# One engine per result slot in the last stage, and three queues for a closing store

## The chip, the cores and the metric

The kernel runs on one core of one Trainium2 chip. The core has TensorE (matrix multiplication into PSUM), VectorE, ScalarE, GpSimd and SyncE, which work in parallel, each on its own queue of instructions, and 16 DMA engines that move data between the device memory and the on-chip memory SBUF. The metric is the device time of one execution in microseconds (us), given as the median of several runs.

In the rows of the profile PE is TensorE, PEld its weight loads, DVE is VectorE, ACT ScalarE, POOL GpSimd and SP SyncE. A q behind the name (SPq, POOLq) is that engine's sequencer, which also issues transfers.

## What is computed

For an input `x` of 2048 positions by 640 channels the reference blends two branches with a gate per position:

```python
g = _sigmoid((x * gate_w).sum(-1, keepdims=True))
a = _A_ref(x, A_wqkv, A_wo)          # dilated sliding-window attention, 32 heads, window 8, projected by wo
b = _B_ref(x, B_A_re, ..., B_Dskip)  # state-space kernel K[d, l], long convolution of x with K by FFT, + x * Dskip
return g * a + (1 - g) * b
```

The last operation concerns us: `g * a` has been computed and stored earlier, the long convolution `b` comes out of the last inverse transform, and `(1 - g) * b + g * a` is formed and stored as bf16.

## The kernel before

The first and longest part computes the gate, the attention branch and the convolution kernel. It leaves `g * a` in a scratch tensor `gaS` in device memory and `1 - g` in `omS`. The second part is `fft_conv` (from line 987): it transforms both factors of the convolution, multiplies the spectra on VectorE, and transforms back in two steps. The step before the last (line 1075) fills slots `cp` in PSUM, which ScalarE and VectorE empty in turn through the helper `evict` (lines 490 to 494) into `C`, a view of the buffer `bufA`.

The last stage is the loop that begins at line 1084. The 32 values of an index `v` are split into ten groups of three and one of two, n = 0 to 10. For each group TensorE fills a PSUM slot `yp` (24 matmuls for three values, line 1105). The slot takes two PSUM banks, and there are four slots. Of each group:

- the first value is finished by VectorE in one fused instruction (`both`, line 1121): it reads the slot, multiplies by `1 - g` (a scalar per partition, `om32`), adds `g * a` (`gaF`) and writes the result tile `ot`;
- the other values are scaled by ScalarE (`scale`, line 1114): one instruction per value reads the slot, multiplies by `1 - g` and writes a tile `tt` in SBUF;
- VectorE then adds `g * a` to the values in `tt` (`mix`, line 1118, one instruction for both values) and writes them to `ot`.

Both engines thus read every slot. A tile `ot` has room for six values and there are four such buffers. Groups 0, 9 and 10 have a tile of their own; groups 1 and 2, 3 and 4, 5 and 6, 7 and 8 share one. When a tile is complete, it is stored in four transfers, one for each 32 partitions: two issued by SyncE and two by GpSimd (line 1132). A transfer of six values moves 120 KB, of three 60 KB, of two 40 KB.

The order of the instructions on each engine is set by a small planner (class `Plan`, lines 69 to 204). Every step is added with an engine, an assumed duration, the steps it depends on, the slots it takes (`acq`) and frees (`rel`) and a due time. The planner simulates the engines with these durations and writes the steps in the order found. On each engine that order is then fixed; the waits between engines and on transfers are put in by the framework, from which tiles an instruction reads and writes.

Of the kernel before, what the change touches and what calls it, by code (L numbers as in the profile page):

```python
# [10 lines left out]
ACT = mybir.ActivationFunctionType  # L11
ALU = mybir.AluOpType
AX = mybir.AxisListType
F32 = mybir.dt.float32
BF16 = mybir.dt.bfloat16
# [5 lines left out]
S = 2048  # L21
D = 640
# [14 lines left out]
def _attn_consts():  # L37
# [5 lines left out]
    for wp in range(W):  # L43
# [7 lines left out]
            v=[299.2, -444.8, 725.4, 80.9, 775.3, 1122.6, -30.6, 686.6], g=[-162.9, 197.0, 381.2, -256.7, -603.2, -606.7, -146.9, -1.6, 186.6, -1231.8, -442.2],  # L51
# [860 lines left out]
def _fft_consts():  # L912
    w = lambda e: np.exp(-2j * np.pi * e / NF)
    t1 = np.arange(32); t2 = np.arange(64); f1 = np.arange(32); f2 = np.arange(64)
    F1 = w(64 * np.outer(t1, f1 + 0.5))
    f1c = np.zeros((32, 32, 2), np.float32)
    f1c[:, :, 0] = F1.real; f1c[:, :, 1] = F1.imag
    f1b = np.zeros((4, 32, 4, 64), np.float32)
    for g in range(4):
        f1b[g, :, (0, 2, 1, 3)[g], :] = f1c.reshape(32, 64)  # L920
    f1c = f1b.reshape(128, 256)
    Phi = w(t2[None, :, None] * (f1[:, None, None] + 0.5 + 64 * f2[None, None, :]))
    phis = np.zeros((64, 2, 32, 3, 2, 64), np.float32)
    for c2 in range(2):
        phis[:, c2, :, 0, c2, :] = Phi.real.transpose(1, 0, 2)
        phis[:, c2, :, 1, c2, :] = Phi.imag.transpose(1, 0, 2)
        phis[:, c2, :, 2, c2, :] = -Phi.imag.transpose(1, 0, 2)
    phis = phis.reshape(128, 32, 3, 128)
    G = np.conj(w(64 * np.outer(f2, t2)))
    ga = np.concatenate([G.real, G.imag], axis=1)  # L930
    gb = np.concatenate([-G.imag, G.real], axis=1)
    gab = np.stack([ga, gb], axis=1)
    gab = np.concatenate([gab, gab], axis=0).astype(np.float32)
    Psi = np.conj(w((64 * t1[None, None, :] + t2[:, None, None]) * (f1[None, :, None] + 0.5))) * (2.0 / NF)
    psis = np.stack([Psi.real, -Psi.imag], axis=-1).transpose(1, 0, 3, 2)
    ps = np.zeros((2, 2, 32, 64, 2, 2, 32), np.float32)
    for e in range(2):
        ps[:, e, :, :, :, e, :] = psis[None]
    psis = ps.reshape(128, 64, 2, 64)
    return f1c.astype(NPBF), phis.astype(NPBF), gab.astype(NPBF), psis.astype(NPBF)  # L940
# [47 lines left out]
def fft_conv(ctx, tc, P, big, Bu, gaS, out2d):  # L988
    nc = tc.nc
    _, _, _, psi_np = _fft_consts()  # L990
# [7 lines left out]
    om32 = sb.tile([128, 32], F32, name="om32")  # L998
    psi = sb.tile([128, 64, 2, 64], BF16, name="psi")
    nc.vector.tensor_copy(om32[:], omF[:])  # L1000
    gaF = P["pool"].tile([128, 32, 320], BF16, name="gaF", tag="uga")
    gr = gaS.rearrange("(a j v) (e c) -> j e a v c", j=2, v=32, e=2)
    orr = out2d.rearrange("(a j v) (e c) -> j e a v c", j=2, v=32, e=2)
    phis, q = P["phis"], {}
    a, b, c = ExitStack(), ExitStack(), ExitStack()
    wk = a.enter_context(tc.tile_pool(name="ff_wk", bufs=2, side="right"))
    q["ps"] = b.enter_context(tc.tile_pool(name="ff_ps2", bufs=2, space=PSUM))
    pl = Plan(free=dict(P=0.0, A=0.0, D=0.0, S=0.0, G=0.0), phase=0.0, look=0.0, ba=0.0, bd=0.0, grace=0.0, warm=1)
    ends, muls = [], {}
    for fb in range(8):  # L1010
        spec, sp = {}, {}
        for n, (nm, ro) in enumerate((("k", 0), ("k", 1), ("u", 0), ("u", 1))):
# [17 lines left out]
            d = 5.2 * fb + 1.3 * n  # L1030
            m = pl.add(f"fp{fb}{nm}{ro}", "P", 1.18, trans, acq=["fp"], due=d)
            e = sp[nm, ro] = pl.add(f"sp{fb}{nm}{ro}", "A", 1.17, ev, deps=[m], rel=[("fp", m)], due=d)
# [10 lines left out]
        t = {}  # L1043
# [12 lines left out]
        for k, (x0, x1) in enumerate(((0, 16), (16, 48), (48, 80)) if fb == 7 else ((0, 80),)):  # L1056
            w = 0.04 + 0.0096 * (x1 - x0)
# [5 lines left out]
    cps, prev = [], None  # L1063
    for cb in range(20):
        ms = []
        for ro in range(2):
# [10 lines left out]
            prev = pl.add(f"inv{cb}{ro}", "P", 0.27, inv, deps=[muls[cb, ro]], after=ends + [prev], acq=["cy"] if ro == 0 else [], due=60 + cb + 0.1 * ro)  # L1077
# [2 lines left out]
        def ev(en, cb=cb):  # L1080
            evict(nc, en, C.rearrange("p x (c q) -> p x c q", c=2)[:, :, :, 4 * cb:4 * cb + 4], q["cp", cb][:].rearrange("p c l x -> p x c l"))
        cps.append(pl.add(f"cp{cb}", "AD", {"A": 1.0, "D": 1.18}, ev, deps=ms, rel=[("cy", ms[0])], due=60 + cb))
    prev, v0 = None, 0
    for n, w in enumerate((3,) * 10 + (2,)):
        vs = range(v0, v0 + w)
        v0 += w
        sole = n in (0, 9, 10)
        if sole or n % 2:
            os, o = [], {"v": vs[0], "n": 0}
        k0 = o["n"]  # L1090
        o["n"] += w

        def fin(_, n=n, vs=vs, o=o, k0=k0):
            if n == 0:
                a.close(); big.close(); c.close()
                q["yps"] = ctx.enter_context(tc.tile_pool(name="ff_ps4", bufs=4, space=PSUM))
                q["wk"] = ctx.enter_context(tc.tile_pool(name="ff_wk2", bufs=4, side="right"))
            if k0 == 0:
                o["t"] = q["wk"].tile([128, 6, 320], BF16, name="ot")
            yp = q["yp", n] = q["yps"].tile([128, 2, 512], F32, name="yp")  # L1100
            for k, v in enumerate(vs):
                for ro in range(2):
                    for j in range(2):
                        for h in range(2):
                            nc.tensor.matmul(yp[64 * j:64 * j + 64, h, 160 * k:160 * k + 160], psi[64 * h:64 * h + 64, 32 * j + v, ro, :], C[64 * h:64 * h + 64, 64 * ro + 32 * j + v, :],
                                             start=(ro == 0), stop=(ro == 1), skip_group_check=True, tile_position=(64 * h, 64 * j))

        def part(k, n=n):
            return q["yp", n][:, :, 160 * k:160 * k + 160]

        def scale(_, v, k, n=n, part=part):
            if k == 1:
                q["tt", n] = q["wk"].tile([128, 2, 320], BF16, name="tt")
            nc.scalar.activation(q["tt", n][:, k - 1, :].rearrange("p (h d) -> p h d", h=2), part(k), ACT.Identity, scale=om32[:, v:v + 1])  # L1114

        def mix(_, n=n, vs=vs, o=o, k0=k0):
            w = len(vs)
            nc.vector.tensor_tensor(o["t"][:, k0 + 1:k0 + w, :], q["tt", n][:, 0:w - 1, :], gaF[:, vs[1]:vs[0] + w, :], ALU.add)  # L1118

        def both(_, v=vs[0], o=o, k0=k0, part=part):  # L1120
            nc.vector.scalar_tensor_tensor(o["t"][:, k0, :].rearrange("p (h d) -> p h d", h=2), part(0), om32[:, v:v + 1], gaF[:, v, :].rearrange("p (h d) -> p h d", h=2), ALU.mult, ALU.add)  # L1121
        m = prev = pl.add(f"yp{n}", "P", 0.20 * w, fin, deps=cps, after=[prev] + (ends + list(muls.values()) if n == 0 else []), acq=["yp"], due=100 + n)
        os.append(pl.add(f"st{n}", "D", 0.47, both, deps=[m], rel=[("yp", m)], due=100 + n))
        tts = []
        for k in range(1, w):
            tts.append(pl.add(f"tt{n}{k}", "A", 0.44, lambda _, f=scale, v=vs[k], k=k: f(_, v, k), deps=[m], acq=["tt"] if k == 1 else [], rel=[("yp", m)], due=100 + n))
        os.append(pl.add(f"mx{n}", "D", 0.46, mix, deps=tts, rel=[("tt", tts[0])], due=100 + n))
        if sole or n % 2 == 0:
            def store(e, o=o):
                for h in range(2):  # L1130
                    j = (0, 2)[e == "G"] + h
                    (nc.sync if e == "S" else nc.gpsimd).dma_start(orr[j // 2, j % 2][:, o["v"]:o["v"] + o["n"], :], o["t"][32 * j:32 * j + 32, 0:o["n"]])  # L1132
            for e, t_ in (("S", 1.3), ("G", 1.1)):
                pl.add(f"out{n}{e}", e, t_, store, deps=os, due=100 + n, dma=0.12 * o["n"])
    pl.emit(tc)


# [5 lines left out]
def gated_mix_kernel(ctx, tc, A_x, A_wqkv, A_wo, B_A_re, B_A_im, B_B_re, B_B_im, B_C_re, B_C_im, B_log_dt, B_Dskip, gate_w, out):  # L1143
# [47 lines left out]
    with c2:  # L1191
# [70 lines left out]
        for n in range(2 * HC):  # L1262
            first("fk", lambda: half[1, "kc"], Bk[:, HC:], n, half[1, "ld"] + [cst], kg.pqs + xdone, pr["u0"] - 50.0 + n)
        pl.emit(tc)
    fft_conv(tc, P, big, now["big"][:].rearrange("p (c f q g) -> p c f q g", c=NCH, f=64, q=8), gaS, o2)


# [50 lines left out]
```

## Time and profile before

| | |
|---|---|
| median of 3 runs | 378.2 us (378.02 to 378.23) |
| the profiled execution | 377.12 us, span 375.1 us |
| busy share: TensorE, VectorE, ScalarE, GpSimd | 84%, 85%, 82%, 26% |
| start of the last stage's matmuls | 354.82 us |
| last result written by VectorE | 369.34 us |
| end of the span | 375.1 us |

The span is the time from the first to the last instruction of the profiled execution; its run took 2.0 us more than its span. A row of the timeline gives start, duration, engine, line, operation, output and inputs, count, and in brackets the idle time before it with what ended that. A row of the groups gives the count, the busy time and the mean of one in ns, then the idle time before them. A row of the windows gives a stretch of the span, the busy time and count of each engine, TensorE's granted clock, the busy share of the DMA engines and the GB/s that they moved.

### The profile page before, as it was taken

To read this page: it belongs to the slowest core of one execution; us is meant where nothing else is said; L and a number is where in the kernel's file an instruction comes from. 1 tells how busy PE (TensorE), PEld (TensorE's weight loads), DVE (VectorE), ACT (ScalarE), POOL (GpSimd) and SP (SyncE) were. 2 spreads that over 40 slices of the span, in tenths; PEclk is the share of its full clock that TensorE was granted. 3 is DMA by queue.
4 is the path that set the end of the run, shared out by engine and by line. 5 is a ranking of instruction groups with operands and counts; after the bars stand their busy time and mean duration, and the time that the engine had idled before them with its cause. 6 is when DMAs were issued, how large, how long until landed. Compare 5 with 4: busy or idle time off the path is not lost. (4 is left out here: it accounts for less than half of the span.)

```text
span 375.1 us, 11789 instructions
## 1 busy us (share of the span) xinstructions
PE 315.3 (84%) x5066; PEld 186.9 (50%) x5094; DVE 320.1 (85%) x436; ACT 307.3 (82%) x415; POOL 95.7 (26%) x129
## 2 busy tenths in 40 slices
PE   0159999998999999979888979999999899997840
PEld 0135664434444455544444445556776665656730
DVE  4698999759999887998999999999897478998872
ACT  1598985389998898897998899997886799996872
POOL 8930450230102113293540201000010032200044
PEclk9998999999999999995969999999999999998995
DMA  8991799671416539605557751311372059932055
GB/s 262 370 252 55 227 284 270 175 231 33 146 62 190 184 101 252 142 17 127 143 127 243 194 187 58 120 56 48 126 249 78 35 134 243 217 79 46 3 135 149
DMA packets 44424, 56.71 MB, mean 151 GB/s; under 512 B 23716, under 2 KB 36580, under 8 KB 44116
## 3 DMA queue, kind: packets, MB, share of 16 engines
q0 software_dynamic: 8112, 28.75, 26.2%
q1 hardware_dynamic: 34804, 26.69, 26.1%
q8 instruction: 40, 0.66, 0.7%
q10 hardware_dynamic: 1456, 0.52, 0.6%
q14 instruction: 12, 0.10, 0.1%
HBM read 36.17 MB, written 19.77 MB: 149 GB/s over the span
## 5 line engine op out<-in xcount | busy, mean ns | idle before, releaser
L330 PE MATMUL tb<-bufA 128*128 128x512 bf16 x283 | 71.2, 388 | 4.5 <-DVE bufA L494 2.3
L772 PE MATMUL ar<-Rarg,L 64*128 64x304 bf16 (+1 forms) x480 | 55.8, 288 | 11.0 <-ACT big L784 4.7
L784 ACT ACTIVATE big<-ar 128x608 bf16<-128x608 int16 x96 | 58.3, 682 | 3.1 <-PE ar L772 2.5
L379 DVE TENSOR_TENSOR prod<-qc,kc 128x2048 bf16<-128x2048 bf16 x40 | 47.4, 1219 | 3.7 <-PE lg L385 3.1
L444 DVE TENSOR_TENSOR pv<-vc,asb 128x2048 bf16<-128x2048 bf16 x40 | 47.3, 1219 | 3.3 <-PE tb L449 3.3
L786 ACT ACTIVATE big<-ar 128x864 bf16<-128x864 f32 x60 | 49.3, 895 | 0.7 <-PE ar L772 0.4
L330 PEld LDWEIGHTS <-bufA 128*128 128x128 bf16 x300 | 33.2, 120 | 31.6 <-issue 6.8
L772 PEld LDWEIGHTS <-L 64*128 64x128 bf16 x480 | 22.3, 95 | 41.8 <-issue 38.0
L449 PE MATMUL tb<-pv,ident 128*128 128x512 bf16 (+1 forms) x181 | 39.7, 356 | 1.0 <-issue 0.5
L825 PE MATMUL kps<-qq,pt 128*32 128x22 bf16 (+1 forms) x2560 | 36.8, 174 | 0.7 <-issue 0.6
L825 PEld LDWEIGHTS <-pt 128*32 128x32 bf16 (+1 forms) x2560 | 25.0, 93 | 23.9 <-issue 15.3
L1021 PEld LDWEIGHTS <-PHI 128*128 128x128 bf16 x256 | 24.8, 97 | 17.7 <-issue 8.3
L492 ACT ACTIVATE prj<-tb 128x512 bf16<-128x512 f32 x27 | 16.0, 598 | 13.8 <-PE tb L330 13.4
L466 PE MATMUL tb<-wo_sb,oT 128*128 128x320 bf16 x160 | 27.2, 300 | 0.0
L449 PEld LDWEIGHTS <-ident 128*128 128x128 bf16 x192 | 18.2, 101 | 14.4 <-issue 2.2
L492 ACT ACTIVATE sp_k<-fp 128x1280 bf16<-128x1280 f32 x16 | 19.4, 1236 | 3.0 <-PE fp L1021 2.5
L245 PE MATMUL ar<-ident,xn 128*128 128x128 bf16 x80 | 7.9, 263 | 16.0 <-DMA xn<-in_A_x_dram 14.3
L809 DVE TENSOR_TENSOR qq<-big 128x1408 bf16<-128x1408 bf16 x24 | 21.2, 884 | 0.0
L1021 PE MATMUL fp<-bufA,PHI 128*128 128x320 bf16 x128 | 19.4, 298 | 2.1 <-ACT sp_u L492 1.2
L1021 PE MATMUL fp<-big,PHI 128*128 128x320 bf16 x128 | 19.5, 298 | 1.6 <-ACT sp_k L492 1.3
L492 ACT ACTIVATE sp_u<-fp 128x1280 bf16<-128x1280 f32 x16 | 19.4, 1236 | 1.6 <-PE fp L1021 1.2
L968 POOL COPY pace<-Usb 32x2 bf16<-32x2 bf16 x7 | 13.2, 1883 | 23.9 <-DMA Usb<-in_A_x_dram 23.9
(168 smaller groups left out, 595.9 us busy)
## 6 DMA issues: line engine op xcount, KB each, us to landing
asb<-aS SPq DMA_DIRECT2D x8, 512.0 KB, 3.9
PHI<-c_phi POOLq DMA_DIRECT2D x8, 384.0 KB, 4.9
Sprm<-pc SPq DMA_DIRECT2D x12, 240.0 KB, 7.6
L<-Sprm SPq DMA_DIRECT2D x80, 36.0 KB, 3.3
kc<-kS POOLq DMA_DIRECT2D x8, 337.5 KB, 6.3
vc<-vS POOLq DMA_DIRECT2D x8, 337.5 KB, 5.2
xn<-in_A_x_dram SPq DMA_DIRECT2D x4, 640.0 KB, 11.6
qc<-qS POOLq DMA_DIRECT2D x8, 320.0 KB, 6.0
```

The source lines that it names most:

```text
L330: nc.tensor.matmul(ppf, self.wq[:, kt, which * D + e:(which + 1) * D:5], self.xT[:, c0 // 1024, kt, c0 % 1024:c0 % 1024 + SC], start=(kt = ...
L379: nc.vector.tensor_tensor(b[e][:], b["qc"][:, e, :].unsqueeze(1).to_broadcast([128, W, C]), win(b["kc"][:, e, :], 0, W, DIL, C), ALU.mult)
L444: nc.vector.tensor_tensor(b["pv", e][:, :, k, :].rearrange("p w (b t) -> p w b t", t=64), for_e, aw, ALU.mult)
L449: nc.tensor.matmul(b["op", e][:, 0:n, :], ident[:], b["pv", e][:, w, 0:n, :], start=(w == 0), stop=(w == W - 1))
L466: nc.tensor.matmul(apf[:, :320], b["oT"][:, e, i * 128:(i + 1) * 128], wo_sb[:, e, hf * 320:(hf + 1) * 320], start=(e == 0), stop=(e == 4))
L492: nc.scalar.activation(o, i, ACT.Identity)
L772: nc.tensor.matmul(ar[:, g2, a0:a0 + ncol], L[rows, sb, gp, l0:l0 + 128], R[rows, c0:c0 + ncol], start=True, stop=True, tile_position=(64 ...
L784: nc.scalar.activation(dst[:, 2 * gp:2 * gp + 2, sub, :], ar[:].bitcast(I16)[:, :, 0:2 * SW:2], ACT.Sin, scale=SCL)
L786: nc.scalar.activation(dst[:, 2 * gp:2 * gp + 2].rearrange("p g s n -> p g (s n)"), ar[:, :, 0:2 * EW], ACT.Exp)
L809: nc.vector.tensor_tensor(qq[:], trg[:, :, KI:].rearrange("p a (v m) -> p a v m", v=2), exq[:, :, KI:].unsqueeze(2).to_broadcast([128, 32, ...
L825: nc.tensor.matmul(kps[32 * g:32 * g + 32, h, NM * ql:NM * ql + NM], pt[rows, k, v, :], qq[rows, k, v, :], start=(g not in started), stop= ...
L1021: nc.tensor.matmul(fp[:, fl, 0:320].rearrange("p (c x) -> p c x", x=32), phis[fb][:, fl, kind, :], B[:, :, 2 * f1 + ri].rearrange("p c q g ...
```

## The change

A slot is emptied by one engine alone. ScalarE takes groups 0, 2, 3, 5, 6, 8 and 9: it scales all three values into a `tt` tile that is now three values wide, and VectorE adds `g * a` to the three in one instruction. VectorE takes groups 1, 4, 7 and 10: it finishes each of their values with the fused instruction, straight from the slot. Result tiles are now closed after groups 1, 3, 5, 7, 9 and 10, so that five hold six values and the last holds two. The store of group 10 is issued by SyncE (one transfer), GpSimd (one) and ScalarE (two); the others as before by SyncE and GpSimd, two each. The durations told to the planner change with the steps. The four `yp`, `tt` and `ot` buffers remain four each.

```diff
-    prev, v0 = None, 0
-    for n, w in enumerate((3,) * 10 + (2,)):
+    prev, v0, os, o = None, 0, [], None
+    for n, (w, own, close) in enumerate(((3, "A", 0), (3, "D", 1), (3, "A", 0), (3, "A", 1), (3, "D", 0), (3, "A", 1), (3, "A", 0), (3, "D", 1), (3, "A", 0), (3, "A", 1), (2, "D", 1))):
...
-        sole = n in (0, 9, 10)
-        if sole or n % 2:
-            os, o = [], {"v": vs[0], "n": 0}
+        o = o or {"v": vs[0], "n": 0}
...
-        def scale(_, v, k, n=n, part=part):
-            if k == 1:
-                q["tt", n] = q["wk"].tile([128, 2, 320], BF16, name="tt")
-            nc.scalar.activation(q["tt", n][:, k - 1, :].rearrange("p (h d) -> p h d", h=2), part(k), ACT.Identity, scale=om32[:, v:v + 1])
+        def scale(_, n=n, vs=vs):
+            q["tt", n] = q["wk"].tile([128, 3, 320], BF16, name="tt")
+            for k, v in enumerate(vs):
+                nc.scalar.activation(q["tt", n][:, k, :].rearrange("p (h d) -> p h d", h=2), q["yp", n][:, :, 160 * k:160 * k + 160], ACT.Identity, scale=om32[:, v:v + 1])
 
         def mix(_, n=n, vs=vs, o=o, k0=k0):
-            w = len(vs)
-            nc.vector.tensor_tensor(o["t"][:, k0 + 1:k0 + w, :], q["tt", n][:, 0:w - 1, :], gaF[:, vs[1]:vs[0] + w, :], ALU.add)
-
-        def both(_, v=vs[0], o=o, k0=k0, part=part):
-            nc.vector.scalar_tensor_tensor(o["t"][:, k0, :].rearrange("p (h d) -> p h d", h=2), part(0), om32[:, v:v + 1], gaF[:, v, :].rearrange("p (h d) -> p h d", h=2), ALU.mult, ALU.add)
+            nc.vector.tensor_tensor(o["t"][:, k0:k0 + len(vs), :], q["tt", n][:, 0:len(vs), :], gaF[:, vs[0]:vs[0] + len(vs), :], ALU.add)
+
+        def both(_, n=n, vs=vs, o=o, k0=k0):
+            for k, v in enumerate(vs):
+                nc.vector.scalar_tensor_tensor(o["t"][:, k0 + k, :].rearrange("p (h d) -> p h d", h=2), q["yp", n][:, :, 160 * k:160 * k + 160], om32[:, v:v + 1],
+                                               gaF[:, v, :].rearrange("p (h d) -> p h d", h=2), ALU.mult, ALU.add)
...
-        os.append(pl.add(f"st{n}", "D", 0.47, both, deps=[m], rel=[("yp", m)], due=100 + n))
-        tts = []
-        for k in range(1, w):
-            tts.append(pl.add(f"tt{n}{k}", "A", 0.44, lambda _, f=scale, v=vs[k], k=k: f(_, v, k), deps=[m], acq=["tt"] if k == 1 else [], rel=[("yp", m)], due=100 + n))
-        os.append(pl.add(f"mx{n}", "D", 0.46, mix, deps=tts, rel=[("tt", tts[0])], due=100 + n))
-        if sole or n % 2 == 0:
-            def store(e, o=o):
-                for h in range(2):
-                    j = (0, 2)[e == "G"] + h
-                    (nc.sync if e == "S" else nc.gpsimd).dma_start(orr[j // 2, j % 2][:, o["v"]:o["v"] + o["n"], :], o["t"][32 * j:32 * j + 32, 0:o["n"]])
-            for e, t_ in (("S", 1.3), ("G", 1.1)):
+        if own == "D":
+            os.append(pl.add(f"st{n}", "D", 0.48 * w, both, deps=[m], rel=[("yp", m)], due=100 + n))
+        else:
+            v = pl.add(f"tt{n}", "A", 0.45 * w, scale, deps=[m], acq=["tt"], rel=[("yp", m)], due=100 + n)
+            os.append(pl.add(f"mx{n}", "D", 0.70, mix, deps=[v], rel=[("tt", v)], due=100 + n))
+        if close:
+            def store(e, o=o, qs="SGAA" if n == 10 else "SSGG"):
+                for j in range(4):
+                    if qs[j] == e:
+                        {"S": nc.sync, "G": nc.gpsimd, "A": nc.scalar}[e].dma_start(orr[j // 2, j % 2][:, o["v"]:o["v"] + o["n"], :], o["t"][32 * j:32 * j + 32, 0:o["n"]])
+            for e, t_ in (("S", 1.3), ("G", 1.1)) + ((("A", 0.8),) if n == 10 else ()):
                 pl.add(f"out{n}{e}", e, t_, store, deps=os, due=100 + n, dma=0.12 * o["n"])
+            os, o = [], None
```

The planner's order for the changed stage is, on ScalarE, the scalings of groups 0, 2, 3, 5, 6, 8, 9 and then the two transfers of group 10; on VectorE group 1, addition 0, group 4, additions 2, 3, 5, group 7, additions 6 and 8, group 10, addition 9. On SyncE and GpSimd the store of group 10 stands before that of groups 8 and 9.

More of the change, by code (lines that the diff above doesn't have):

```diff
@@ L1106, in fin @@
                                              start=(ro == 0), stop=(ro == 1), skip_group_check=True, tile_position=(64 * h, 64 * j))
-        def part(k, n=n):
-            return q["yp", n][:, :, 160 * k:160 * k + 160]
-        def scale(_, v, k, n=n, part=part):
-            if k == 1:
-                q["tt", n] = q["wk"].tile([128, 2, 320], BF16, name="tt")
-            nc.scalar.activation(q["tt", n][:, k - 1, :].rearrange("p (h d) -> p h d", h=2), part(k), ACT.Identity, scale=om32[:, v:v + 1])
```

## The prediction

> **What bounds the kernel now.** I read the chain that ended last first, then the waits of the stretch that the diff touches, then the timeline of each engine there, then the transfers. The profiled execution spans 375.1 us and took 377.12 us as a run; the median of the three runs shown is 378.2 us. The chain, in order of time, between 366 us and the end, cut:
>
> ```profile
> 366.43 0.53 ACT tt L1114
> 366.96 0.03 issue
> 366.99 0.56 DVE ot L1121
> 367.55 0.03 issue
> 367.57 0.02 ACT tt L1114
> ...
> 370.09 1.08 POOL out_dram L1132 x2
> 371.17 0.53 POOLq L1313
> ```
>
> ScalarE and VectorE hand one slot back and forth, and then GpSimd issues the last transfers. The waits from 354 to 376 us say the same (us in total, times, longest):
>
> ```profile
> PE yp L1105 <- ACT tt L1114: 3.0, 7, 0.6
> ACT tt L1114 <- DVE ot L1121: 3.0, 6, 0.7
> DVE ot L1121 <- ACT tt L1114: 2.2, 3, 1.0
> POOL out_dram L1132 <- issue: 0.8, 1, 0.8
> ```
>
> ScalarE waits 3.0 us for VectorE and VectorE 2.2 us for ScalarE, though neither needs the other's result there: both only read the same PSUM slot. TensorE, too, waits 3.0 us for ScalarE to free a slot. The stage's groups between 353 and 372 us (count | busy us, mean ns):
>
> ```profile
> L1114 ACT ACTIVATE tt<-yp,om 128x320 bf16<-128x320 f32 x21 | 9.8, 524 | 4.1 <-DVE ot L1121 3.0 <-PE yp L1105 1.0
> L1121 DVE SCALAR_TENSOR_TENSOR ot<-yp,om,gaF 128x320 bf16<-128x320 f32 x11 | 5.9, 547 | 3.8 <-ACT tt L1114 2.2 <-issue 1.6
> L1118 DVE TENSOR_TENSOR ot<-tt,gaF 128x640 bf16<-128x640 bf16 x10 | 4.9, 489 | 0.7 <-ACT tt L1114 0.4
> L1118 DVE TENSOR_TENSOR ot<-tt,gaF 128x320 bf16<-128x320 bf16 x1 | 0.3, 315 | 0.0
> ```
>
> The stage computes from 355.64 to 369.34 us (last row below, 369.02 + 0.32), 13.7 us, with 9.8 us of ScalarE work. The rows of the timeline from which starts and pitches come:
>
> ```profile
> 354.82 1.97 PE L1105 MATMUL yp<-bufA,psi 64*64 64x160 bf16 x96 [1.29 <-DVE bufA L494]
> 355.64 0.53 ACT L1114 ACTIVATE tt<-yp,om 128x320 bf16<-128x320 f32 x1 [1.04 <-PE yp L1105]
> 356.27 1.01 DVE L1121 SCALAR_TENSOR_TENSOR ot<-yp,om,gaF 128x320 bf16<-128x320 f32 x2 [1.59 <-issue]
> 357.43 0.61 PE L1105 MATMUL yp<-bufA,psi 64*64 64x160 bf16 x24 [0.64 <-ACT tt L1114]
> 366.01 0.95 ACT L1114 ACTIVATE tt<-yp,om 128x320 bf16<-128x320 f32 x2 [0.62 <-DVE ot L1121]
> 368.13 0.49 DVE L1118 TENSOR_TENSOR ot<-tt,gaF 128x640 bf16<-128x640 bf16 x1 [0.20 <-ACT tt L1114]
> 368.55 0.55 DVE L1121 SCALAR_TENSOR_TENSOR ot<-yp,om,gaF 128x320 bf16<-128x320 f32 x1
> 369.02 0.32 DVE L1118 TENSOR_TENSOR ot<-tt,gaF 128x320 bf16<-128x320 bf16 x1
> 369.54 2.16 POOL L1132 DMA_DIRECT2D out_dram<-ot  x4 [0.18 <-DVE ot L1118]
> ```
>
> Behind the computing stand the transfers: issues with KB each and us from issue to landing (the first two in the tail from 345 us, then the one issued at 362.20 us, the one at 368.79 us, the last two of the run, and the spread over GpSimd's fourteen), and the windows of the tail, whose last two columns are the busy share of the 16 DMA engines and GB/s:
>
> ```profile
> out_dram<-ot SPq DMA_DIRECT2D x8, 120.0 KB, 2.5
> out_dram<-ot POOLq DMA_DIRECT2D x8, 120.0 KB, 3.2
> ...
> out_dram<-ot POOLq DMA_DIRECT2D x1, 120.0 KB, 4.1
> ...
> out_dram<-ot POOLq DMA_DIRECT2D x1, 120.0 KB, 3.5
> ...
> out_dram<-ot POOLq DMA_DIRECT2D x2, 40.0 KB, 2.6
> ...
> DMA to landing us min/median/max: 2.0/3.0/4.1
> ```
>
> ```profile
> 364.50:367.50 3.00, 0.00 (x0) 0.00 (x0) 1.77 (x5) 1.83 (x4) 1.13 (x2) 0.62 0.70 181
> 367.50:370.00 2.50, 0.00 (x0) 0.00 (x0) 1.64 (x5) 0.94 (x2) 1.59 (x3) 0.50 0.56 126
> 370.00:372.50 2.50, 0.00 (x0) 0.00 (x0) 0.00 (x0) 0.00 (x0) 1.70 (x4) 0.50 0.95 265
> 372.50:375.10 2.60, 0.00 (x0) 0.00 (x0) 0.00 (x0) 0.00 (x0) 0.00 (x0) 0.50 0.05 16
> ```
>
> The last GpSimd issue begins at 371.17 us and lands 2.6 us later, at 373.77; the span ends 1.36 us after that landing. I take these 1.36 us (closing waits and barrier) as fixed.
>
> **The change part by part.** Everything before line 1083 is left alone, so the stage starts at the same 355.64 us.
>
> Tile by tile ownership: ScalarE's 21 scalings stay 21, now three to a slot (slots 0, 2, 3, 5, 6, 8, 9). VectorE's fused instructions stay 11 (slots 1, 4, 7, 10), and its 11 additions become 7 of 128x960. No slot is read by both, so the 3.0 and 2.2 us of waits lose their cause. ScalarE: two in one slot take 0.95 us, so the pitch is 0.95 - 0.53 = 0.42 and three take 0.42 x 2 + 0.53 = 1.37 us; seven slots take 9.6, from 355.64 to 365.2 us, if TensorE is always ahead. It is: slots 0 to 3 are filled by 356.79 (354.82 + 1.97), every later one in 0.61 us once its slot is free, and slot 5, wanted by ScalarE at 359.7, follows VectorE's reading of slot 1, over at 357.6.
>
> VectorE's addition of 960 columns is not in the trace: from 315 ns at 320 and 489 at 640 the straight line gives 663 ns. Bounds: 489 x 2 = 978 ns above, 489 below; I take 663, nearest to the measured slope. A fused triple has a pitch of 1.01 - 0.55 = 0.46 and takes 0.46 x 2 + 0.55 = 1.47 us. In the order that the planner writes (slot 1, add 0, slot 4, add 2, add 3, add 5, slot 7, add 6, add 8, slot 10, add 9), with starts overlapping by 0.08 us as at 368.13 to 368.55: slot 1 ends 357.6, add 0 at 358.2, slot 4 at 359.6, add 2 at 360.2, add 3 at 360.8; add 5 waits for ScalarE's 361.1 and ends 361.8; slot 7 at 363.2, add 6 at 363.8, add 8 (waits for 363.84) at 364.5. Four adds fewer is worth 0.6 us of VectorE work (7 x 663 = 4.6 against 5.2), and lies inside its waiting.
>
> New order at the end: slot 10 stands before add 9 on VectorE, and its result tile is the sixth of four buffers, so it waits for the store of slots 2 and 3 to land, with add 9 queued behind it. That store is issued on GpSimd from 360.8 + 0.2 = 361.0, its second transfer at 361.55 (0.54 us an issue, 2.16/4), landing 3.2 us later, at 364.75, so slot 10 runs 364.75 to 365.8 and add 9 ends at 366.35. If it lands as quickly as 2.6 us, slot 10 starts at 364.5 when VectorE is free, and add 9 ends at 366.1; as slowly as 4.1, at 367.25. Computing ends 3.0 us earlier than 369.34 (2.1 to 3.2).
>
> Transfers: 28 issues become 24 (GpSimd 11, SP 11, ScalarE 2), the bytes are the same. Slots 9 and 10 used to close last with 240 and 160 KB; now the 160 KB store of slot 10 goes out first, over SP, GpSimd and twice ScalarE, and the 480 KB store of slots 8 and 9 follows last, over SP and GpSimd only, past that store on both queues. On GpSimd: slot 10 at 366.0 to 366.55, the last two issues at 366.55 and 367.1. ScalarE has its last two issues after its scalings and nothing queued behind them. Their price late in the run isn't in the trace; those at the start are the nearest rows:
>
> ```profile
> L568 ACTq DMA_DIRECT2D bre<-in_B_B_re_dram x1: 525/525/525, 1.1 to 1.1; - x1
> L568 ACTq DMA_DIRECT2D bim<-in_B_B_im_dram x1: 548/548/548, 1.7 to 1.7; - x1
> ```
>
> I take 0.55 us each: from 365.8 they end at 366.9, and with the median landing of 3.0 us the second lands at 369.35, ahead of the last of GpSimd below, so they cost nothing (below, nothing either; above, 1.25 us more, 1.8 for the first issue, before they set the end). The last GpSimd transfer: 367.1 + 3.5 us (its size in the crowded tail; 3.2 to 4.1) = 370.6, plus 1.36 = 372.0 us. The volume checks this. The stores that start at 360.8 (480 KB), 361.8 (480), 363.8 (480), 366 (160) and 366.4 (480) keep the engines busy from about 361.3 on; at the 265 GB/s of the full window 2.1 MB (2080 KB x 1.024) take 8.0 us, to 369.3; at 236 or so, a tenth lower, 9.0 us, to 370.3; the span end is 2.5 us behind the last data (372.6 to 375.1), so 371.8 to 372.8. The two give 372.0 and 372.3; I take 372.2, 2.9 us under 375.1. The profiled run would be 374.2, and the median 378.2 - 2.9 = 375.3 us.
>
> The page "DMA: Bandwidth & Descriptors" of the Trainium skill, section "Issuing engines are not separate DMA queues", says that transfers from all issuing engines share the same 16 DMA engines, and that a further issuer saves only issuing time. By that rule the third queue is worth the one GpSimd issue it replaces, 0.55 us, and no bandwidth; the share of 0.95 with two queues agrees. The sum above counts it so, and by the rule too the median is 375.3 us. As the computing ends earlier, the rule speaks for rival 1.
>
> **The rivals.** (1) The drain becomes the bound at a lower rate. For it: between 364.5 and 367.5 the engines moved 181 GB/s at a share of 0.70. Against: they were waiting for issues then. At 181 GB/s the 2.1 MB from 361.3 take 11.8 us, to 373.1, and the span ends at 375.6: median 378.7. That would be the full price, and no window with queued work is so slow; at 220 GB/s the data end at 371.0, the span at 373.5, the median at 376.6, which is what I allow this case. Computing ends earlier and the transfers become the end.
> (2) The slot 10 wait is long. For it: 4.1 us occurred, and GpSimd once stood 0.8 us between two issues. Both together add 0.9 + 0.8 = 1.7 us: 377.0; one alone 376.2.
> (3) The other side, slower: the same place, VectorE standing at slot 10 with add 9 behind it. As it already waits at 3.2 us, each further us of landing is a us of span; the 2.9 us are gone at 3.2 + 2.9 = 6.1 us and it is slower by 0.8 from 6.9 us on, say 379.2 at 7.1. The longest landing of fourteen is 4.1 us.
> (4) No change within what can be told, 378.2: the two engines, reading PSUM at once, slow each other so that scalings take 0.67 us in place of 0.53. Against: in the stage before, both empty PSUM at once, each at its own even pace (two rows below), and the order written for the changed program has the scalings waiting for TensorE.
>
> ```profile
> 348.82 5.86 DVE L494 CAST bufA<-cp 128x1024 bf16<-128x1024 f32 x5
> 349.78 4.82 ACT L492 ACTIVATE bufA<-cp 128x1024 bf16<-128x1024 f32 x5
> ```
>
>
> **How the numbers follow.** Forecast, 374.5 to 376.0: 0.60. Rival 1 at 376 to 377.4: 0.15. Rival 2 at 376.0 to 377.2: 0.12. Rival 4: 0.05. Rival 3: 0.08. Below 374.3 lies only what an early landing (366.1) with 2.6 us of landing at the end would give, 366.85 + 2.6 + 1.36 = 370.8, 374.0 as a median. One part in a hundred of rival 2 is within the bound below. The range 374.2 to 377.1 leaves out rivals 3 and 4 and the edges. A difference of 0.2%, 0.76 us, is about what a measurement of this kernel can tell from none: faster 0.86, same 0.06, slower 0.08.
>
> **What would show it.** Right: no wait of ScalarE's scalings for VectorE or the reverse at the fused instruction; ScalarE's last scaling ends near 365.2, VectorE's last addition near 366.4, an addition takes some 0.66 us; the last GpSimd issue ends near 367.7; the span is near 372.2. Wrong: VectorE idle before slot 10 with a transfer as releaser for over 2 us; additions near 0.98 us; a DMA share near 1 after the last addition at well under 265 GB/s, or a tail after the last landing longer than 1.36 us.

## The result and the profile after

The changed kernel takes 376.42 us (median of 7 runs, 375.34 to 377.2); the kernel before, over as many, 378.2 us (377.63 to 378.4). The ratio is 0.9954, with a 95% interval of 0.994 to 0.9968: faster by 1.8 us, where 2.9 had been forecast. The profiled execution took 376.8 us with a span of 375.0 us, and looks no faster than the one before (377.12 and 375.1); the waits and the timeline show why. First the waits from 354 to 376 us:

```profile
...
POOL out_dram L1128 <- DVE ot L1116: 2.0, 1, 2.0
PE yp L1103 <- ACT tt L1109: 1.8, 4, 0.6
DVE ot L1116 <- DMA out_dram<-ot: 1.6, 1, 1.6
DVE ot L1116 <- PE yp L1103: 1.4, 1, 1.4
...
```

The rows in which ScalarE and VectorE waited for each other (3.0 and 2.2 us) are gone. Two new ones have come: VectorE waits 1.6 us for a store, and GpSimd 2.0 us for the slot that VectorE finishes after it. The stage's groups between 353 and 375 us:

```profile
L1109 ACT ACTIVATE tt<-yp,om 128x320 bf16<-128x320 f32 x21 | 8.9, 597 | 1.0 <-PE yp L1103 1.0
...
L1116 DVE SCALAR_TENSOR_TENSOR ot<-yp,om,gaF 128x320 bf16<-128x320 f32 x11 | 5.4, 544 | 3.0 <-DMA out_dram<-ot 1.6 <-PE yp L1103 1.4
...
L1112 DVE TENSOR_TENSOR ot<-tt,gaF 128x960 bf16<-128x960 bf16 x7 | 4.4, 652 | 0.2 <-issue 0.2
```

And the rows of the timeline that answer to those of before:

```profile
356.87 1.97 PE L1103 MATMUL yp<-bufA,psi 64*64 64x160 bf16 x96 [1.29 <-DVE bufA L494]
357.68 8.90 ACT L1109 ACTIVATE tt<-yp,om 128x320 bf16<-128x320 f32 x21 [1.04 <-PE yp L1103]
...
361.44 1.22 DVE L1112 TENSOR_TENSOR ot<-tt,gaF 128x960 bf16<-128x960 bf16 x2
...
362.95 1.13 POOL L1128 DMA_DIRECT2D out_dram<-ot  x2 [0.97 <-DVE ot L1112]
...
364.86 1.22 DVE L1112 TENSOR_TENSOR ot<-tt,gaF 128x960 bf16<-128x960 bf16 x2
367.70 1.01 DVE L1116 SCALAR_TENSOR_TENSOR ot<-yp,om,gaF 128x320 bf16<-128x320 f32 x2 [1.62 <-DMA out_dram<-ot]
368.62 0.65 DVE L1112 TENSOR_TENSOR ot<-tt,gaF 128x960 bf16<-128x960 bf16 x1
368.74 0.86 ACTq L1128 DMA_DIRECT2D out_dram<-ot  x2
369.00 0.57 POOL L1128 DMA_DIRECT2D out_dram<-ot  x1 [2.03 <-DVE ot L1116]
369.84 1.15 POOL L1128 DMA_DIRECT2D out_dram<-ot  x2 [0.27 <-issue]
```

The stage begins 2.05 us later in this execution (first matmul at 356.87 instead of 354.82), with the same instructions ahead of it. That hides the gain in the spans. From here on I therefore measure the stretch from the stage's first matmul to the end of the span, 20.28 us before and 18.13 us after, and split it at the end of VectorE's last instruction: 14.52 + 5.76 us before, 12.40 + 5.73 us after. Of the 2.15 us 2.12 come from the computing; what follows it costs the same.

The chain that ended last, of after, passes through GpSimd:

```profile
366.40 0.57 POOL out_dram L1128
366.97 2.02 issue
368.99 0.02 POOLq L1128
369.00 0.56 POOL out_dram L1128
369.56 0.27 issue
369.84 0.58 POOL out_dram L1128
370.42 0.56 POOLq L1310
```

GpSimd stands 2 us idle for slot 10, which stands for the landing of the store of slots 2 and 3. The landings, as the spread over the transfers of the store line whose landing the profile records and as the median of GpSimd's last two:

```profile
DMA to landing us min/median/max: 2.2/3.3/4.1
...
out_dram<-ot POOLq DMA_DIRECT2D x2, 120.0 KB, 3.2
```

Two of the profiles used below, marked with an asterisk, are of slow executions, over 1.5% above the fastest of their kernel; they serve as second looks only.

### The profile page after: what moved, and what is told of

Its sections match the earlier page's. It is cut to its first block, busy times and chain, and to the rows that moved or that the text cites. A ratio compares the mean times of both kernels' runs of the same rounds, so it can differ in the third digit from the quotient of the medians.

```text
span 375.0 us, 11773 instructions
## 1 busy us (share of the span) xinstructions
PE 317.9 (85%) x5066; PEld 185.7 (50%) x5094; DVE 319.5 (85%) x432; ACT 307.2 (82%) x415; POOL 93.1 (25%) x126
## 5 line engine op out<-in xcount | busy, mean ns | idle before, releaser
L330 PE MATMUL tb<-bufA 128*128 128x512 bf16 x283 | 73.0, 394 | 3.9 <-DVE bufA L494 1.5
L772 PE MATMUL ar<-Rarg,L 64*128 64x304 bf16 (+1 forms) x480 | 57.5, 296 | 9.6 <-ACT big L784 3.9
L825 PEld LDWEIGHTS <-pt 128*32 128x32 bf16 (+1 forms) x2560 | 25.1, 93 | 25.7 <-issue 17.4
L1021 PE MATMUL fp<-big,PHI 128*128 128x320 bf16 x128 | 19.5, 298 | 1.5 <-ACT sp_k L492 1.1
L370 POOL DMA_DIRECT2D vc<-vS x8 | 7.5, 936 | 47.4 <-DVE pv L444 38.3
```

The lines of the kernel that those rows point to most:

```text
L330: nc.tensor.matmul(ppf, self.wq[:, kt, which * D + e:(which + 1) * D:5], self.xT[:, c0 // 1024, kt, c0 % 1024:c0 % 1024 + SC], start=(kt = ...
L772: nc.tensor.matmul(ar[:, g2, a0:a0 + ncol], L[rows, sb, gp, l0:l0 + 128], R[rows, c0:c0 + ncol], start=True, stop=True, tile_position=(64 ...
L825: nc.tensor.matmul(kps[32 * g:32 * g + 32, h, NM * ql:NM * ql + NM], pt[rows, k, v, :], qq[rows, k, v, :], start=(g not in started), stop= ...
L1021: nc.tensor.matmul(fp[:, fl, 0:320].rearrange("p (c x) -> p c x", x=32), phis[fb][:, fl, kind, :], B[:, :, 2 * f1 + ri].rearrange("p c q g ...
```

## The experiments

Two theories for the missing 0.75 us of the stage. A: the wait of slot 10, with addition 9 behind it. B: the drain, that is the time that the DMA engines need to move what has been issued to them; the 16 engines are nearly full once the stores follow each other closely. All variants leave the instructions ahead of the stage as they are. Their times were taken beside the kernel before on the same chip, and there they spread by several us, more than the variants differ among themselves: the intervals of the variants of the changed kernel all overlap with its own, and by the first median of six tiles alone (374.47 us, where the kernel before had 377.64) theory A would have won. The profiles decide, also where an expectation names medians: in the 14 of them the first matmul of the stage came between 354.8 and 361.7 us, while the kernel before had a stretch of 20.28 and 20.29 us. The numbers of all, in us:

| kernel | first matmul to last VectorE result | from there to the end | stretch | ratio of times to before (95%) |
|---|---|---|---|---|
| forecast | 11.53 | 5.85 | 17.38 | 0.992 |
| before | 14.52 | 5.76 | 20.28 | |
| before, again | 14.49 | 5.80 | 20.29 | |
| changed | 12.40 | 5.73 | 18.13 | 0.9954 (0.994 to 0.9968) |
| changed, again* | 13.09 | 5.68 | 18.77 | 0.9929 (0.9891 to 0.9966) |
| six tiles* | 10.67 | 6.96 | 17.63 | 0.9914 (0.9883 to 0.9944) |
| six tiles, again | 10.68 | 6.76 | 17.44 | 0.9946 (0.9923 to 0.9968) |
| two queues | 13.01 | 5.78 | 18.79 | 0.9942 (0.9909 to 0.9975) |
| third queue alone | 14.51 | 6.15 | 20.66 | 1.004 (1.0014 to 1.0066) |
| third queue alone, again | 14.50 | 6.29 | 20.79 | 1.0027 (0.9997 to 1.0057) |
| addition 9 first | 12.44 | 5.28 | 17.72 | 0.9929 (0.9898 to 0.996) |
| six tiles, addition 9 first | 11.30 | 6.71 | 18.01 | 0.9924 (0.9889 to 0.9958) |
| first store early | 10.34 | 8.06 | 18.40 | 0.9943 (0.9909 to 0.9976) |
| half of the stores | 11.55 | 4.82 | 16.37 | 0.9918 (0.9888 to 0.9949) |
| ownership alone | 12.93 | 5.79 | 18.72 | 0.9944 (0.9915 to 0.9974) |

### Six result tiles

```diff
-                o["t"] = q["wk"].tile([128, 6, 320], BF16, name="ot")
+                o["t"] = q["wk"].tile([128, 6, 320], BF16, name="ot", bufs=6)
```

> The changed kernel with six result tiles in place of four, so that slot 10 no longer waits for the store of slots 2 and 3. Theory A (that wait, 1.62 us in the profile, with addition 9 queued behind it, is what the forecast lacked): addition 9 ends about 10.0 us after the first scaling in place of 11.6, the span ends 1.3 to 1.6 us earlier, median 374.8 to 375.1 us. Theory B (the 16 DMA engines are nearly full from 364.5 us on, and the bytes and the time of the first store set the end): addition 9 ends as early, but the span ends at most 0.5 us earlier, median 375.9 to 376.4 us, and the last store takes longer from its issue to landing.

> Six result tiles once more, as its profile began late and its runs were few. The stretch from the first matmul to the end is 17.4 to 18.0 us again (17.6; the changed kernel had 18.1 and 18.8), addition 9 ends some 9.9 us after the first scaling, and the ratio to the kernel before is 0.991 to 0.995. Should the wait have been the whole price, the stretch would be 16.4 to 16.9 us.

The timeline of the second run:

```profile
365.44 1.22 DVE L1112 TENSOR_TENSOR ot<-tt,gaF 128x960 bf16<-128x960 bf16 x2
366.57 1.00 DVE L1116 SCALAR_TENSOR_TENSOR ot<-yp,om,gaF 128x320 bf16<-128x320 f32 x2
367.49 0.65 DVE L1112 TENSOR_TENSOR ot<-tt,gaF 128x960 bf16<-128x960 bf16 x1
...
368.71 1.14 POOL L1128 DMA_DIRECT2D out_dram<-ot  x2 [0.28 <-issue]
```

Slot 10 follows the additions without a pause; the wait is gone, and VectorE ends 1.7 us earlier than in the changed kernel (10.68 against 12.40). The end moves by 0.7 us only (17.44 against 18.13): what follows the computing grows from 5.73 to 6.76 us. The wait had a price, 0.7 us, and the other 1 us of it was covered by the drain. Against the two other profiles with this wait (18.77* and 18.79 us) the price is 1.3 to 1.4 us; how much of that is spread the runs do not show. The second expectation held: 17.44 us, and 9.87 us from the first scaling to the end of addition 9. The windows, taken at the same distances from the first scaling (2.5 to 6, 6 to 9, 9 to 12 and 12 to 14.5 us behind it; the last two columns are DMA share and GB/s), in the changed kernel:

```profile
360.18:363.68 3.50, 2.33 (x101) 1.76 (x96) 3.26 (x7) 3.50 (x10) 1.89 (x4) 1.00 0.61 148
363.68:366.68 3.00, 0.47 (x16) 0.28 (x15) 2.39 (x5) 2.90 (x7) 2.37 (x5) 0.99 0.90 234
366.68:369.68 3.00, 0.00 (x0) 0.00 (x0) 1.57 (x3) 0.00 (x0) 0.85 (x2) 0.50 0.91 255
369.68:372.18 2.50, 0.00 (x0) 0.00 (x0) 0.00 (x0) 0.00 (x0) 1.15 (x2) 0.50 0.88 226
```

and with six tiles:

```profile
360.77:364.27 3.50, 2.33 (x101) 1.76 (x96) 3.27 (x7) 3.50 (x10) 1.88 (x4) 1.00 0.62 147
364.27:367.27 3.00, 0.47 (x16) 0.28 (x15) 3.00 (x7) 2.88 (x7) 2.36 (x5) 1.00 0.91 232
367.27:370.27 3.00, 0.00 (x0) 0.00 (x0) 0.87 (x2) 0.00 (x0) 2.00 (x4) 0.74 0.98 262
370.27:372.77 2.50, 0.00 (x0) 0.00 (x0) 0.00 (x0) 0.00 (x0) 0.00 (x0) 0.50 0.96 255
```

With six tiles the engines are busy at 0.96 to 0.98 after the computing and move 255 to 262 GB/s: here the drain is what holds up the end; the next run tests that.

### Half of the stores

```diff
-            def store(e, o=o, qs="SGAA" if n == 10 else "SSGG"):
+            def store(e, o=o, qs="S-A-" if n == 10 else "S-G-"):
```

> The changed kernel with only half of each store issued (the first and the third transfer of four; half of the output is not written): the same computing, half the bytes. Theory B: the stretch from the first matmul to the end falls by 2 us or more, to 15.5 to 16.1 us (addition 9 at 10.7, then issue, landing and closing as in the trace of the kernel before, 0.2 + 0.6 + 2.6 + 1.4, with the wait of slot 10 gone too). Theory A: as with six tiles without a wait, 16.4 to 16.9 us; if neither matters, 18.

```profile
359.84:363.34 3.50, 2.32 (x101) 1.76 (x96) 3.27 (x7) 3.50 (x10) 1.17 (x2) 1.00 0.39 83
363.34:366.34 3.00, 0.47 (x16) 0.28 (x15) 2.38 (x5) 2.88 (x7) 1.14 (x2) 0.98 0.77 179
366.34:369.34 3.00, 0.00 (x0) 0.00 (x0) 1.57 (x3) 0.00 (x0) 0.14 (x1) 0.50 0.51 116
369.34:371.84 2.50, 0.00 (x0) 0.00 (x0) 0.00 (x0) 0.00 (x0) 0.43 (x1) 0.50 0.33 67
```

The stretch is 16.37 us, somewhat above what theory B named (15.5 to 16.1) as slot 10 still waited 0.8 us for a store, and 1.1 us under that of six tiles, although VectorE ends 0.9 us later. What follows the computing falls to 4.82 us, with a DMA share of 0.33 in its last window. Half of the issues are gone too, but that is not what shortens the end: GpSimd's last issue begins some 1.1 us after VectorE's last result in all three kernels (here without a reason that the profile shows), and its 120 KB land in 2.3 us here, 3.2 in the changed kernel and 3.8 with six tiles. The wait of slot 10 depends on the load as well, 0.8 us with half of the bytes against 1.6. So both theories hold, one behind the other: the wait first, then the drain.

### Two queues for all stores

```diff
-            def store(e, o=o, qs="SGAA" if n == 10 else "SSGG"):
+            def store(e, o=o, qs="SSGG"):
```

> The changed kernel with the store of slot 10 over SyncE and GpSimd, two transfers each, as all others: the third queue alone is undone. If it saves issuing time on GpSimd, whose slot 10 issues stand ahead of the last store, the last GpSimd issue starts 0.57 us later and the median is 376.7 to 377.0 us. If the transfers are bound by the DMA engines, no change: 376.2 to 376.6 us. Over 377.2 us would mean that the third queue carries bandwidth of its own.

The stretch is 18.79 us, 0.66 more than with the third queue, but that comes ahead of the store in question: VectorE ends 0.61 us later, as slot 10 waited 2.2 us instead of 1.6. From there to the end it takes 5.78 us against 5.73. The third queue does save an issue: without it GpSimd's last issue begins 0.5 us later after VectorE's end (1.6 us against 1.1). But that transfer then lands in 2.7 us in place of 3.2. In sum the third queue is worth 0.05 us in the changed kernel, which no run here can tell from nothing.

### The third queue alone, on the kernel before

```diff
-            def store(e, o=o):
-                for h in range(2):
-                    j = (0, 2)[e == "G"] + h
-                    (nc.sync if e == "S" else nc.gpsimd).dma_start(...)
-            for e, t_ in (("S", 1.3), ("G", 1.1)):
+            def store(e, o=o, qs="SGAA" if n == 10 else "SSGG"):
+                for j in range(4):
+                    if qs[j] == e:
+                        {"S": nc.sync, "G": nc.gpsimd, "A": nc.scalar}[e].dma_start(...)
+            for e, t_ in (("S", 1.3), ("G", 1.1)) + ((("A", 0.8),) if n == 10 else ()):
```

> The kernel before with only the store of the last slot changed to one transfer on SyncE, one on GpSimd and two on ScalarE. There the last GpSimd issue is the end of the chain: if issuing time counts, one issue of 0.54 us less gives 377.5 to 377.8 us. If the transfers are bound by the DMA engines: 378.0 to 378.3 us.

> The third queue alone on the kernel before, once more: the first time its stretch from the first matmul to the end was 20.7 us against 20.3, and its ratio 1.004. If the third queue costs something, it is 20.5 to 21 us again and the ratio over 1.002; if that was the spread of what lies before the stage, 20.0 to 20.5 us and a ratio of 0.997 to 1.002.

Neither forecast of the first run held: it is slower. The second run came as expected for a queue that costs something (20.79 us, ratio 1.0027), though the interval of its times just reaches 1. The computing is the same (14.5 us), and what follows it takes 6.15 and 6.29 us, where the kernel before takes 5.76 and 5.80. GpSimd's last issues and their landings, of the kernel before in its second profile:

```profile
372.03 2.15 POOL L1132 DMA_DIRECT2D out_dram<-ot  x4 [0.21 <-DVE ot L1118]
...
out_dram<-ot POOLq DMA_DIRECT2D x2, 60.0 KB, 3.0
out_dram<-ot POOLq DMA_DIRECT2D x2, 40.0 KB, 2.6
```

and with the third queue in its second profile:

```profile
373.92 1.62 POOL L1132 DMA_DIRECT2D out_dram<-ot  x3 [0.19 <-DVE ot L1118]
...
out_dram<-ot POOLq DMA_DIRECT2D x2, 60.0 KB, 3.7
out_dram<-ot POOLq DMA_DIRECT2D x1, 40.0 KB, 3.6
```

GpSimd is done 0.53 us earlier, as one issue is gone, but its last transfer lands 1.0 us later after its issue. ScalarE's first transfer is issued at 373.74 us, and from 374.21 to 375.21 us the DMA share is 0.99. That its transfers go ahead of part of what GpSimd has issued, and displace it, is argued from these rows, not shown by a run of its own.

### Addition 9 ahead of slot 10

```diff
-            os.append(pl.add(f"st{n}", "D", 0.48 * w, both, deps=[m], rel=[("yp", m)], due=100 + n))
+            os.append(pl.add(f"st{n}", "D", 0.48 * w, both, deps=[m], after=[os9] if n == 10 else [], rel=[("yp", m)], due=100 + n))
...
+            os9 = os[-1]
             os, o = [], None
```

> The changed kernel with four result tiles, but addition 9 ahead of slot 10 on VectorE, so that the 480 KB store of slots 8 and 9 is not behind the wait and the 160 KB store of slot 10 goes last over three queues. Theory A: addition 9 ends about 9.6 us after the first scaling, slot 10 still ends at about 11.0, the span ends about 1.5 us earlier: median 374.6 to 375.2 us. Theory B: at most 0.5 us earlier, 375.9 to 376.4 us.

> The changed kernel with six result tiles and addition 9 ahead of slot 10: no wait on a store is left and the small store goes last. Theory A (the wait was the price): the stretch from the first matmul to the end is 16.4 to 16.9 us, 1.2 to 1.7 less than the changed kernel's 18.1. Theory B (the 16 DMA engines, full from about 6 us after the first scaling, are the end): 17.4 to 17.8 us, as in the two kernels that took only one of the two steps (17.6 and 17.7).

Four tiles in this order give 17.72 us, 0.4 less than the changed kernel: the last store is small again, and what follows VectorE's end falls to 5.28 us, although slot 10 still waits 1.0 us for a store. With six tiles besides no wait on a store is left, and it is 18.01 us: nothing is gained by it. Neither reaches theory A's time. The first gains no more than theory B allowed (0.5 us); the second is 0.2 us above the 17.4 to 17.8 us of theory B, about as much as the two profiles of six tiles alone lie apart.

### The first store early

```diff
-    ... ((3, "A", 0), (3, "D", 1), (3, "A", 0), (3, "A", 1), (3, "D", 0), (3, "A", 1), (3, "A", 0), (3, "D", 1), (3, "A", 0), (3, "A", 1), (2, "D", 1)) ...
+    ... ((3, "D", 1), (3, "A", 0), (3, "A", 1), (3, "D", 0), (3, "A", 1), (3, "A", 0), (3, "D", 1), (3, "A", 0), (3, "A", 1), (3, "D", 0), (2, "A", 1)) ...
```

(with six tiles)

> Six result tiles, and the closings moved: slot 0 goes to VectorE and is stored alone, slots 1 and 2, 3 and 4 and so on together, so that the first store is issued about 1.2 us earlier; the bytes are the same. Theory B: the transfers start earlier, so the end moves with them: the stretch from the first matmul to the end 16.5 to 17.1 us, some 0.5 to 1.1 under the 17.6 of six tiles alone. Theory A: nothing is gained over six tiles alone, 17.5 to 17.8 us.

18.40 us, 1 us more than six tiles alone in its second profile, so the forecast of theory B failed here; but the test isn't clean. The first store came earlier (2.46 us after the first matmul against 3.35) and was half as large, and the next one came 2.5 us behind it, no sooner than with six tiles alone, as on VectorE additions 1 and 2 stand behind slot 3. From 5 to 7 us after the first matmul the DMA share was 0.49, against 0.82 with six tiles alone, so the DMA engines ran short of work between the two stores. It is inconclusive on whether an earlier start helps.

### Ownership alone

```diff
-    ... ((3, "A", 0), (3, "D", 1), (3, "A", 0), (3, "A", 1), (3, "D", 0), (3, "A", 1), (3, "A", 0), (3, "D", 1), (3, "A", 0), (3, "A", 1), (2, "D", 1)) ...
+    ... ((3, "A", 1), (3, "D", 0), (3, "A", 1), (3, "A", 0), (3, "D", 1), (3, "A", 0), (3, "A", 1), (3, "D", 0), (3, "A", 1), (3, "A", 1), (2, "D", 1)) ...
-            def store(e, o=o, qs="SGAA" if n == 10 else "SSGG"):
+            def store(e, o=o, qs="SSGG"):
```

> One engine per slot as in the changed kernel, but result tiles closed as in the kernel before (slots 0, 9 and 10 alone, the others in pairs) and two queues for all stores. If the ownership carries the gain, the waits between ScalarE and VectorE are gone, and the stretch from the first matmul to the end is 17.6 to 18.6 us against 20.3 before and 18.1 to 18.8 for the whole change. If the larger first and last stores carry it, 19.5 us or more.

18.72 us, 0.1 over the range that was expected if the ownership carries the gain, and far from 19.5: 1.6 of the 2.15 us. Its waits hold no row of ScalarE for VectorE either, and slot 10 stands just as long for a store:

```profile
DVE ot L1116 <- DMA out_dram<-ot: 1.7, 1, 1.7
```

The rest between it and the changed kernel, 0.6 us, is no more than the changed kernel's first profile and that of two queues lie apart (18.13 and 18.79), so what the larger first and last stores bring is not shown.

### The two kernels again

> The changed kernel once more, beside the kernels below on one chip. If the stretch from the stage's first matmul to the end of the span is the same from run to run and the rest of the spread comes from before the stage, that stretch is again 17.9 to 18.4 us (18.1 in its first profile, 20.3 in the kernel before), and the ratio is 0.993 to 0.997.

The changed kernel's second profile came out at 18.77 us, outside the stretch expected: slot 10 stood 2.3 us for the store, 0.7 more than the first time. In the kernel with two queues, whose instructions are the same up to the store of slot 10, it was 2.2 us. This wait is the part that varies (1.6 to 2.3 us); what follows the computing stays at 5.68 to 5.78.

> The kernel before once more, for a second profile of its last stage. If the stage repeats itself and the spread of the times comes from before it, the stretch from the stage's first matmul to the end of the span is again 20.0 to 20.6 us (20.3 in the first profile), whenever the stage begins.

The kernel before repeats to 0.01 us, with a stage that began 2.5 us later.

## Why the prediction was right or wrong

- **The hand-over between ScalarE and VectorE: right.** Its waits are gone, and alone it brings 1.6 us. ScalarE's 21 scalings took 8.90 us, and 9.6 had been forecast: the pitch of 0.42 us holds across slots too, where I had counted a full 0.53 us at the end of each. Nothing came of that: VectorE was free for slot 10 at 8.40 us after the first scaling in place of 8.86, and then stood for the store.
- **The addition of 960 columns: right**, 652 ns against 663.
- **The wait of slot 10 for its result tile: right as a place, wrong in its price.** This is the term that failed. It was priced with a landing of 3.2 us, the median of GpSimd's 120 KB transfers. The second transfer of slots 2 and 3 was issued at about 363.52 (362.95 and one issue) and VectorE went on at 367.70, so 4.2 us, of which the landing is 4.0. The row for it was on view: the one transfer of 4.1 us, from the crowded stretch at 362.2 us, which I kept as the upper end. With it, the same working gives the last addition 0.9 us later, and it came 0.87 us later (12.40 against 11.53). Rival 2 was this, and took the forecast's place. Of the 1.1 us by which the median lies above 375.3, this stage has 0.75 us in its profile; the other 0.35 us are within what the part ahead of the stage varies by, and the runs do not show more of them.
- **The transfers at the end: right in sum, by luck.** 5.85 us forecast, 5.73 measured, with two errors that cancel: slot 10's store held up GpSimd's last issue by 0.4 us more (1.15 us from VectorE's end to the start of the last issue, and 0.75 forecast), and its landing was quicker than 3.5 us. The run that puts the small store last again was 0.4 us shorter, less than the changed kernel's two profiles lie apart.
- **Drain as the end (rival 1): not in this kernel, but next in line.** With the wait gone, a longer drain eats 1 us of 1.7. It is not wholly apart from rival 2, which the prediction priced separately: with half of the bytes the wait itself fell to 0.8 us. The Trainium skill, "DMA: Bandwidth & Descriptors", section "Issuing engines are not separate DMA queues", has it that a further issuing engine saves only issuing time. The runs agree that it brings no bandwidth: in the changed kernel it saved 0.5 us of issuing, and the end came no sooner (5.73 against 5.78 us). They go further: on the kernel before it cost 0.4 to 0.5 us, issuing time saved and all.
- **Rivals 3 and 4: did not come.** The longest landing in the changed kernel was 4.1 us, and 4.7 in its second profile, and the scalings' pitch did not grow.

## What to carry to other kernels

When two engines read the same PSUM slot, look for waits between them in the rows of both; giving each slot to one engine removed them here, with no more instructions than before. Price a wait on a transfer from the row of a transfer under the same load, not from the median, and ask which buffer that transfer frees and what stands behind its waiter on the engine. When computing near the end of a kernel is shortened, look at the DMA share of the last windows: near 1, as with six tiles here, fewer bytes shortened the end and a shorter computation did so in part only. Whether moving the same bytes sooner helps was left open here.

## What the runs showed of the hardware

- ScalarE's scalings of 128x320 from PSUM, following each other at once, were recorded longer than their pitch: 597 ns on average, with 21 of them in 8.90 us (0.42 us each).
- Stores of 640-byte rows reached 255 to 262 GB/s at a share of 0.96 to 0.98 of the 16 engines (six tiles, second profile).
- A store of 120 KB issued by GpSimd landed in 2.4 us as GpSimd's first of the stage, and in 4.0 us as the eighth transfer of that size, issued 2.7 us later (changed kernel).
- A third issuing queue late in the drain, at a DMA share of 0.97 and 0.99, made the stretch of the kernel before 0.4 to 0.5 us longer, in both profiles (20.66 and 20.79 us against 20.28 and 20.29).
- The part ahead of the stage, the same instructions in all, ended between 354.8 and 361.7 us. The clock granted to TensorE differs between these executions (mean 0.939 to 0.960), but does not order them: the profile with 0.960 began the stage at 359.3 us, the one with 0.952 at 356.9. What else does is left open.
